# Infini-attention with a gating MLP: three units of stacks, maxima seven steps ahead, two products of w1 ahead, gates in one transfer

## The chip, the cores and the metric

The kernel runs on one core of a Trainium2 chip. A core has five engines that run side by side, each with its own stream of instructions in order: TensorE (PE in the profile, with its weight loads as PEld), VectorE (DVE), ScalarE (ACT), GpSimd (POOL) and SyncE (SP), which here only issues transfers (DMAs). The metric is the device time of one launch in microseconds; several runs are taken and their median counts.

## The reference, cut to what matters

```python
def _A_ref(x, wq, wk, wv, wo, beta):            # x: 1 x 2048 x 512
    H = 32; Dh = 16; N = 4; L = 512             # 4 segments of 512 rows
    q, k, v = (x @ w split into 32 heads and 4 segments, for w in wq, wk, wv)
    g = _sigmoid(beta)                          # one gate per head
    for s in range(N):
        p = _softmax(qs @ ks.T * Dh**-0.5 + causal mask)
        a_dot = p @ vs
        a_mem = (phi(qs) @ M) / (phi(qs) @ z + 1e-6)
        outs.append(g * a_mem + (1 - g) * a_dot)
        M += phi(ks).T @ vs;  z += sum(phi(ks))  # phi(t) = t + 1 if t > 0 else exp(t)
    return concat(outs) @ wo

def _B_ref(x, w1, w2):                           # 512 -> 1792 -> 512
    return max(x @ w1, 0) @ w2

xn = _layernorm(x)
return x + _A_ref(xn, ...) * _silu(_B_ref(xn, w1, w2))
```

## The kernel before

**Numbers.** Each dense product is made of three matmuls on operands split into a rounded part (h) and the rest (l): h·h, h·l, l·h. `triple` (L791) issues such a product, `lanes` (L744) cuts each of its matmuls into two of 64 rows, a lower and an upper one, which run on the two halves of the array side by side. The upper halves are held back: they trail the lower ones by up to `BACK` = 14 matmuls, so a chain of products ends 14 steps after its last lower half. The planner counts 0.69 us (`M3`) for a triple. ACT makes the rounded part of a weight (L475), POOL the rest (L476).

**Work.** The 2048 rows are 4 segments; the 512 columns of a segment's q or k are 4 groups of 8 heads, so there are 16 groups n, each in two units u = 2n + q of 4 heads, 32 units in all.

- `proj` (L1004) makes q and k of a group; `projout` (L1017) splits them and writes them to DRAM planes sdq and sdk (L1031, L1032): 0 or -1, then h and l.
- `stack` (L1161) loads a unit's planes into one of `NS` = 4 pairs of buffers QS and KS, one transfer of 512 KB each (L1167). In them one matmul over 64 rows gives the logits of a head.
- `rowmax` (L1179), five steps per unit: PE makes logits (L1193), DVE takes the maximum of each row over the causal part in one operation that also has to write its elements somewhere: it writes them back into the PSUM bank (L1199). `maxrows` (L1212): POOL splits the maxima (L1207, L1208), DVE transposes them (L1217), SP sends them to DRAM (mx, L1219) and from there into the free rows of the unit's QS (L1220).
- `expo` (L1229), five steps per unit: PE makes the logits again, transposed and now less their maximum (L1245), ACT the exponentials P (L1262, L1256), POOL clears the part above the diagonal (L1252). `pv` (L1275) multiplies by v (L1291) and ACT scales the result by 1 - g (F, L1306, with gsc).
- `memory`, `memory2`, `spread`, `numden` keep M and z and make the memory's share; its numerator is scaled by g (L1084, L1087, with gcol). `combine` (L1329) sends the denominators through DRAM for their reciprocals (cr, rq, dd, ee) and adds both shares (L1358 to L1363).
- `w1chain` (L807): one of 14 products f of 128 hidden columns, then hh on ACT (L819) and hl on DVE (L820), in rings of `NH` = 4 buffers. `w2chains` (L831) takes them in parts of 3 (the last part has 2), four chains of 128 rows, and adds into bacc (L870, L872). In `filler` (L1428) the w2 chains of a part follow the w1 product number `LOOK` = 1 of the next part.
- `gates` (L428): g from beta in two layouts, gcol (128 x 4) and gsc (128 x 8), loaded by 8 and 4 transfers (L430, L433), then tanh on ACT (L445, L446) and small steps on DVE (L447, L450, L451).
- `wipe` (L856) writes zeros with POOL into buffers whose last readers are lower halves: rows of xh and xl in the last segments, and at the end (L1621) whatever weight or hl buffer is marked in `lowread`.

**Order.** `emit` walks over steps t from -18 to 160. In each it spends a budget of filler work (w1, w2, v, layer norm, the output product), then issues `rowmax` of step t + `LAG` (9), more filler, then `expo` of step t; the exponentials of unit u start at step 5u. For group n, with T = 10n, `proj` is made urgent at T - 17 and the two stacks go out at T - 14 and T - 8. PE's stream is issued as it comes; the operations of ACT, DVE, POOL and SP are put in order by a planner (`Sched`, L73), which runs a model of the engines: each operation has a duration, a latency and a due time, and the engine that is free takes the ready operation that is due first. `await_` (L1507) pushes filler to PE until what a step needs is there by the model. The whole is planned several times, and the order that ends first by the model is the one that is built (`search`, L244). The model of the maxima is

```python
dve(w + 80, [pk, "causal"], ..., lambda ...: DVE.tensor_tensor_reduce(
    pS[:, o:o + w], pS[:, o:o + w], causal[:, L - w:], 1.0, -3.0e38, OP.add, OP.max, md[...]), 4.6)
```

that is 0.14 us and 1.05 ns for each of w + 80 columns. A transfer counts 0.63 us on SP and 2.2 us or a stated time until it has landed.

## Time and profile before

| | |
|---|---|
| median of 3 runs | 779.08 us (777.58, 779.08, 782.65) |
| profiled execution | 777.05 us, span 775.3 us, mean granted clock 0.985 |
| busy share of the span | PE 95%, DVE 63%, ACT 55%, POOL 53% |
| chain that ended last | PE 66%, DMA 15%, DVE 6%, issue 4%, ACT 4%, POOL 4% |
| transfers | 139.87 MB, 127074 packets, 26296 of them under 512 B |
| queue of SP | 56.5% of 16 DMA engines over the span |

The profile names an instruction by its line, engine and tiles (out<-in, buffer numbers left out). A wait "A <- B" is idle time of A that ended when B was done; the three numbers are the total in us, how often, and the longest. SPq and ACTq are the issues of transfers on these engines. Stages are read by their busy time per engine, followed by the clock granted to TensorE (1.00 is full), the share of the DMA engines and the rate.

### The profile page before, as it was taken

What the parts mean: (1) busy time and instruction counts of PE and PEld (TensorE: products, weight loads), DVE (VectorE), ACT (ScalarE), POOL (GpSimd) and SP (SyncE); (2) the same over time, 40 slices, a digit from 0 to 9 for tenths busy, and PEclk for the clock granted to TensorE, in tenths of its full rate; (3) what the DMA queues carried; (4) which work ended last, traced back from release to release, by engine and by line L of the source; (5) the groups of instructions that cost most, each with busy time, mean ns of one, the idle gap of its engine ahead of it and who ended that gap; (6) DMA issues with size and microseconds to landing.
All of it is one profiled execution on the core that took longest, in us unless ns stands there. A gap on an engine that the chain in (4) does not pass through costs nothing.

```text
span 775.3 us, 18578 instructions
## 1 busy us (share of the span) xinstructions
PE 734.1 (95%) x6832; PEld 573.3 (74%) x6832; DVE 486.0 (63%) x1489; ACT 422.8 (55%) x646; POOL 414.0 (53%) x508
## 2 busy tenths in 40 slices
PE   9979999999999999989899989989899999999997
PEld 8868877677777668756687759767666977766776
DVE  3115888588676876456676876367786556684344
ACT  3434455567676565445565765356556456766511
POOL 2734344354555355563664554573838557657652
PEclk9999999999999999989999999999999999999989
DMA  4565754556665456665466556656665847743413
GB/s 134 179 191 178 259 189 136 162 202 195 220 213 176 154 183 196 200 198 142 150 226 221 166 187 221 209 172 194 203 187 180 281 162 251 230 122 90 115 33 109
DMA packets 127074, 139.87 MB, mean 180 GB/s; under 512 B 26296, under 2 KB 71608, under 8 KB 126984
## 3 DMA queue, kind: packets, MB, share of 16 engines
q1 hardware_dynamic: 126776, 138.49, 56.5%
q8 instruction: 54, 0.88, 0.5%
q14 instruction: 36, 0.29, 0.1%
q10 hardware_dynamic: 208, 0.20, 0.1%
HBM read 99.00 MB, written 34.93 MB: 173 GB/s over the span
## 4 chain that ended last, share of the span: by engine, by line
PE 66%; DMA 15%; DVE 6%; issue 4%; ACT 4%; POOL 4%; SPq 1%; POOLq 0%; ACTq 0%; DVEq 0%
PE ps L775 35%; PE ps L784 9%; PE ps L1291 7%; PE pt L1245 4%; DMA sdq<-qkl 4%; PE ps L1193 4%; DMA sdk<-qkl 3%; DVE ps L1199 2%; PE pt L545 2%; DMA gcol<-in_A_beta_dram 2%; DMA ee<-rq 2%; ACT P L1262 1%; PE ps L1075 1%; DVE qkl L1028 1%; DMA io<-in_B_w_dram 1%
## 5 line engine op out<-in xcount | busy, mean ns | idle before, releaser
L476 POOL TENSOR_TENSOR wl<-io,wh 128x512 fp32r<-128x512 f32 x176 | 226.9, 1299 | 148.0 <-ACT wh L475 126.1
L1199 DVE CUSTOM_DVE_ANT_0 ps<-ps,causal 128x256 f32<-128x256 f32 (+3 forms) x512 | 244.0, 510 | 85.9 <-PE ps L1193 66.0
L1262 ACT ACTIVATE P<-pt 128x1024 f32<-128x1024 f32 x128 | 131.1, 1024 | 60.0 <-PE pt L1245 58.4
L1252 POOL TENSOR_SCALAR_AFFINE_SELECT P<-P 128x512 f32<-128x512 f32 x128 | 80.0, 636 | 120.0 <-ACT P L1262 91.7
L775 PE MATMUL ps<-xh,wh 64*128 64x512 f32 x352 | 141.4, 402 | 2.5 <-DVE md L1199 1.7
L784 PE MATMUL ps<-xl,wh 64*128 64x512 f32 x352 | 141.5, 402 | 0.0
L475 ACT ACTIVATE wh<-io 128x512 fp32r<-128x512 f32 x176 | 107.6, 628 | 58.4 <-PE ps L784 28.2
L784 PE MATMUL ps<-xh,wh 64*128 64x512 f32 x352 | 139.1, 395 | 0.0
L784 PE MATMUL ps<-xh,wl 64*128 64x512 f32 x352 | 137.8, 391 | 0.0
L775 PE MATMUL ps<-xh,wl 64*128 64x512 f32 x352 | 137.3, 390 | 0.0
L775 PE MATMUL ps<-xl,wh 64*128 64x512 f32 x352 | 137.0, 389 | 0.0
L775 PE MATMUL ps<-wh,hh 64*128 64x512 f32 x224 | 93.2, 416 | 12.7 <-ACT hh L819 8.6
L784 PE MATMUL ps<-wl,hh 64*128 64x512 f32 x224 | 92.5, 413 | 0.0
L775 PE MATMUL ps<-wh,hl 64*128 64x512 f32 x224 | 90.6, 404 | 0.9 <-DVE hl L820 0.8
L775 PE MATMUL ps<-wl,hh 64*128 64x512 f32 x224 | 89.2, 398 | 0.0
L784 PE MATMUL ps<-wh,hh 64*128 64x512 f32 x224 | 88.4, 395 | 0.0
L784 PE MATMUL ps<-wh,hl 64*128 64x512 f32 x224 | 88.3, 394 | 0.0
L1245 PE MATMUL pt<-qs,ks 64*128 64x128 f32 (+3 forms) x512 | 80.5, 336 | 6.9 <-ACT P L1262 6.8
L1193 PE MATMUL ps<-ks,qs 64*128 64x256 f32 (+3 forms) x512 | 76.8, 326 | 3.8 <-DVE hl L820 2.6
L1291 PE MATMUL ps<-P,vt 128*17 128x512 f32 (+3 forms) x1024 | 75.1, 434 | 1.7 <-POOL P L1252 1.7
L775 PEld LDWEIGHTS ps<-xh,wh 64*128 64x128 f32 x352 | 65.0, 185 | 12.8 <-DVE md L1199 4.4
L1199 DVE DVE_READ_ACCUMULATOR2_ANT md<- 128x1 f32 x512 | 72.1, 141 | 0.0
(175 smaller groups left out, 1789.4 us busy)
## 6 DMA issues: line engine op xcount, KB each, us to landing
io<-in_B_w_dram SPq DMA_DIRECT2D x112, 256.0 KB
qs<-sdq SPq DMA_DIRECT2D x32, 512.0 KB
ks<-sdk SPq DMA_DIRECT2D x32, 512.0 KB
sdq<-qkh SPq DMA_DIRECT2D x16, 512.0 KB
sdk<-qkh SPq DMA_DIRECT2D x16, 512.0 KB
io<-in_A_x_dram SPq DMA_DIRECT2D x28, 256.0 KB
io<-in_A_wv_dram SPq DMA_DIRECT2D x16, 256.0 KB
io<-in_A_wq_dram SPq DMA_DIRECT2D x16, 256.0 KB
```

The source lines that it names most:

```text
L475: act(512, [rk], [hk], lambda: ACT.activation(h, raw, AF.Copy), 7.0 + nsplit if early else 6.0)
L476: pool(512, [rk, hk], [lk], lambda: POOL.tensor_tensor(l, raw, r32(h), op=OP.subtract), 8.5 + 1.3 * nsplit if early else 25.4)
L545: PE.matmul(pw[:, :128], ident, ident, start=True, stop=True)
L775: i = PE.matmul(m[0], m[2][0][LO], m[2][1][LO], start=m[4], stop=False)
L784: PE.matmul(h[0], h[2][0][HI], h[2][1][HI], start=False, stop=h[5] is not None)
L1028: dve(512, [pk, thk], [tlk], lambda: DVE.tensor_tensor(tl, pp, r32(th), op=OP.subtract), 7.0)
L1193: PE.matmul(two[a][0][:, o:o + w], qs[r, p, w - 128:w], ks[r, p, :w], start=True, stop=True)
L1199: dve(w + 80, [pk, "causal"], [f"{dk}.{p}{a}{j}"], lambda p=p, j=j, o=o, w=w, a=a, pS=pS: DVE.tensor_tensor_reduce(pS[:, o:o + w], pS[:, o ...
L1245: PE.matmul(pT[:, a, o:o + w], ks[r, p, 128 * i:128 * i + 128], qs[r, p, 128 * i:], start=True, stop=True)
L1252: pool(512, ks, ks, lambda: POOL.affine_select(t, t, pattern=[[0, 4], [1, 128]], compare_op=OP.is_ge, fill=0.0, base=0, channel_multiplier ...
L1262: act(1024, tk, [both[p]], lambda: ACT.activation(P[:, 2 * p:2 * p + 2, :], pT, AF.Exp, scale=0.25), 18.5)
L1291: PE.matmul(pO[32 * b:32 * b + 17, 128 * i:], v, P[:, b, o:o + w], start=i == 0, stop=i == 3)
```

## The change

Constants: `NH` 4 to 5, `LOOK` 1 to 2, `NS` 4 to 3, `LAG` 9 to 7; new are `LOAD` = 0.11, `STACK` = (-10, -5) and `TTR` = 60.

- One unit of QS and KS less, and the stacks of a group go out at T - 10 and T - 5. The maxima run seven steps ahead of the exponentials, not nine.
- The w2 chains of a part follow the second w1 product of the next part; hh and hl have five buffers.
- The planner counts 0.11 us more until PE can use another engine's result.
- The gates come by one transfer: beta, repeated to all 128 partitions (bt, 128 x 32). One tanh on ACT, then eight small DVE operations (`picks`) choose gcol and gsc by masks made from blk.
- The maxima's operation writes its elements to a BF16 buffer in SBUF (none), and counts as 20 more columns.
- `wipe`, `retire` and `lowread` go.

```diff
-NH = 4
-LOOK = 1
+NH = 5
+LOOK = 2
-NS = 4
+NS = 3
-LAG = 9
+LAG = 7
+LOAD = 0.11
+STACK = (-10, -5)
+TTR = 60
...
             if d.eng != "PE":
-                s = max(s, d.t)
+                s = max(s, d.t + LOAD)
...
             if o is not None and o.eng != "PE":
-                t = max(t, o.t if o.out else self.now + 3.54)
+                t = max(t, o.t + LOAD if o.out else self.now + 3.54)
...
+    none = cst.tile([128, L], BF16, name="none")
...
     def gates():
-        for h in range(8):
-            dma((), [f"gcol{h}"], lambda h=h: SP.dma_start(gcol[16 * h:16 * h + 16], bass.AP(
-                tensor=beta.tensor, offset=beta.offset + h, ap=[[0, 16], [8, 4]])), 55.2)
-        for b in range(4):
-            dma((), [f"gsc{b}"], lambda b=b: SP.dma_start(gsc[32 * b:32 * b + 32], bass.AP(
-                tensor=beta.tensor, offset=beta.offset + b, ap=[[0, 32], [4, 8]])), 35.9)
+        dma((), ["bt"], lambda: SP.dma_start(bt, bass.AP(
+            tensor=beta.tensor, offset=beta.offset, ap=[[0, 128], [1, H]])), 10.0, 4.0)
...
+        def picks():
+
+            DVE.tensor_scalar(bt, bt, 0.5, 0.5, op0=OP.mult, op1=OP.add)
+            DVE.tensor_tensor(pick2, blk[:, 0::32], blk[:, 16::32], op=OP.add)
+            DVE.tensor_tensor(pick1, bt.rearrange("p (c h) -> p c h", h=8),
+                              blk[:, 0::16][:, None, :].to_broadcast([128, 4, 8]), op=OP.mult)
+            DVE.tensor_reduce(gcol, pick1, axis=AX.X, op=OP.add)
+            DVE.tensor_tensor(pick3, bt.rearrange("p (c b) -> p c b", b=4),
+                              pick2[:, None, :].to_broadcast([128, 8, 4]), op=OP.mult)
+            DVE.tensor_reduce(gsc, pick3, axis=AX.X, op=OP.add)
+            DVE.tensor_scalar(gsc, gsc, -1.0, 1.0, op0=OP.mult, op1=OP.add)
+            DVE.tensor_scalar(gsc, gsc, par[:, 1:2], par[:, 0:1], op0=OP.mult, op1=OP.add)
+
         dve(400, ["pari"], ["pari", "par"], parity, 54.1)
-        act(10, gk, gk, lambda: ACT.activation(gcol, gcol, AF.Tanh, scale=0.5), 62.2)
-        act(10, sk, sk, lambda: ACT.activation(gsc, gsc, AF.Tanh, scale=0.5), 77.5)
-        dve(10, gk, gk, lambda: DVE.tensor_scalar(gcol, gcol, 0.5, 0.5, op0=OP.mult, op1=OP.add), 76.6)
...
+        act(10, ["bt"], ["bt"], lambda: ACT.activation(bt, bt, AF.Tanh, scale=0.5), 62.2)
+        S.pend["ACT"][-1].dur = 1.6
+        dve(1000, ["bt", "blk", "par"], ["bt", "gcol", "gsc"], picks, 74.7)
...
-                dve(w + 80, [pk, "causal"], [f"{dk}.{p}{a}{j}"], lambda p=p, j=j, o=o, w=w, a=a, pS=pS: DVE.tensor_tensor_reduce(
-                    pS[:, o:o + w], pS[:, o:o + w], causal[:, L - w:], 1.0, -3.0e38, OP.add, OP.max,
+                dve(w + 40 + TTR, [pk, "causal"], [f"{dk}.{p}{a}{j}"], lambda p=p, j=j, o=o, w=w, a=a, pS=pS: DVE.tensor_tensor_reduce(
+                    none[:, :w], pS[:, o:o + w], causal[:, L - w:], 1.0, -3.0e38, OP.add, OP.max,
...
-            if t == T - 14:
+            if t == T + STACK[0]:
...
-            if t == T - 8:
+            if t == T + STACK[1]:
                 stack(n, 1)
...
-    for t, k in (*WH.t, *WL.t, *HLO.t):
-        if k in lowread:
-            wipe(t, [k])
```

## The prediction, made before the change was run

> **What bounds the kernel now.** I read the page first, then the waits of PE in three stretches, then stages of 20 us, then the places.

> ```profile
> span 775.3 us, 18578 instructions
> PE 734.1 (95%) x6832; PEld 573.3 (74%) x6832; DVE 486.0 (63%) x1489; ACT 422.8 (55%) x646; POOL 414.0 (53%) x508
> ...
> PE ps L775 <- ACT hh L819: 4.6, 1, 4.6
> PE ps L1122 <- ACT bacc L870: 1.7, 1, 1.7
> PE ps L775 <- DVE hl L820: 0.5, 1, 0.5
> ...
> PE pt L1245 <- ACT P L1262: 6.8, 7, 2.8
> PE ps L775 <- DVE md L1199: 4.7, 9, 1.1
> ...
> PE ps L775 <- ACT hh L819: 2.3, 3, 0.9
> ...
> PE ps L775 <- DVE hl L820: 0.3, 1, 0.3
> ...
> PE ps L775 <- ACT hh L819: 1.8, 1, 1.8
> ```

> The first three waits lie in 20 to 70 us, the next four in 70 to 740, the last in 740 to 776 (total us, times, longest). PE is busy 95% of the span and no other engine passes 63%, so PE's stream sets the time: what can be won is its idle 41.2 us (775.3 - 734.1), and the stretches in which it is busy at a low clock. The stages show these:

> ```profile
> 40.00:60.00 20.00, 14.12 (x108) 11.37 (x104) 3.65 (x8) 6.63 (x12) 5.06 (x4) 0.91 0.67 201
> ...
> 340.00:360.00 20.00, 19.86 (x166) 14.80 (x168) 10.60 (x37) 10.79 (x17) 8.02 (x13) 0.84 0.34 106
> 360.00:380.00 20.00, 16.29 (x122) 11.35 (x122) 13.98 (x42) 11.56 (x18) 13.59 (x15) 0.91 0.74 233
> ...
> 740.00:760.00 20.00, 18.20 (x94) 13.84 (x91) 11.37 (x20) 5.52 (x11) 8.14 (x13) 0.83 0.09 22
> ```

> Columns: stretch, length, busy PE, PEld, DVE, ACT, POOL, then granted clock, DMA share, GB/s. A clock of 0.91 over 20 us is 1.8 us of full-speed work lost, 0.84 is 3.2, 0.83 is 3.4. So the opening (40 to 62) loses 4.6 + 0.5 + 1.7 idle and 1.8 by the clock, 8.6 in all; the tail (746 to 756) loses 1.8 idle and 3.4 by the clock, 5.2 in all.

> **Gates by one transfer.** Why PE stands in the opening, and below it two pairs of mx transfers (units 23 and 31 of the 32), each with the last md before it and the first exponential behind it:

> ```profile
> GB/s 154 332 261 336 362 220 204 290 369 235 89 1 0 0 0 0 0 50 263 403 366 173 25 172 342 332 318 308 251 76 154 340 52 264 328 344 391 352 332 206
> ...
> gcol<-in_A_beta_dram SPq DMA_DIRECT2D x8, 0.2 KB
> gsc<-in_A_beta_dram SPq DMA_DIRECT2D x4, 1.0 KB
> ...
> 44.98 1.28 ACT L446 ACT_TABLE_LOAD   x1 [7.73 <-DMA gsc<-in_A_beta_dram]
> ...
> 60.12 0.21 ACT L445 ACTIVATE gcol<-gcol 128x4 f32<-128x4 f32 x1 [5.09 <-DMA gcol<-in_A_beta_dram]
> ...
> 46.73 0.29 DVE L451 TENSOR_SCALAR gsc<-gsc,par 128x8 f32<-128x8 f32 x1
> ...
> 551.02 0.14 DVE L1199 DVE_READ_ACCUMULATOR2_ANT md<- 128x1 f32 x1
> ...
> 556.84 0.41 SPq L1219 DMA_DIRECT2D mx<-mT  x1
> ...
> 561.71 0.59 SPq L1220 DMA_DIRECT2D qs<-mx  x1
> ...
> 567.51 0.50 PE L1245 MATMUL pt<-qs,ks 64*128 64x512 f32 x2
> ...
> 700.57 0.14 DVE L1199 DVE_READ_ACCUMULATOR2_ANT md<- 128x1 f32 x1
> ...
> 701.90 0.33 SPq L1219 DMA_DIRECT2D mx<-mT  x1
> ...
> 703.91 0.59 SPq L1220 DMA_DIRECT2D qs<-mx  x1
> ...
> 713.90 0.50 PE L1245 MATMUL pt<-qs,ks 64*128 64x512 f32 x2
> ```

> The first row is the DMA rate of 25 to 66 us in 40 slices: from 36 to 42 us next to nothing moves. A gsc transfer of 1 KB is 256 pieces of 4 bytes, one of gcol 64, and all else on the queue stands behind them. ACT takes its instructions in order: at L446 it stands 7.73 us, and behind it hh (L819), for which PE then waits 4.6; at L445 it stands 5.09 us, and behind it bacc (L870), for which PE waits 1.7. The change sends 128 rows of 128 bytes once. That is the shape of an mx transfer, whose hop from its issue to the issue that needs it took 2.0 us (701.90 to 703.91) and 4.9 us (556.84 to 561.71). The planner allows 4.0 and 0.63 of issue for it, so ACT waits between 0 and 0.3 us, and the table load of 1.28 us, which the planner had not counted, is in the 1.6 that it now counts. Eleven issues leave SP. On DVE eight small operations (picks) come in; at 0.2 to 0.3 us each, as L451, that is 1.6 to 2.4 us where 0.6 stood. Nothing reads them before the first scaled output (F), and DVE is busy for 3.65 of the 20 us from 40 to 60; without that cover they cost 1.8. I take the whole opening but 0.4: **-8.2** (bounds -4, if another late input stops ACT at the same place, and -8.6).

> **w1 two products ahead of w2.** Today the w2 chains of a part start when one w1 product of the next part is through, and the last hh that they need ends within them, since the upper halves trail by up to 14 steps where a product has 12. Hence L775's waits on hh and hl of 2.3 + 0.3 us in mid-run. In the tail w1 of f = 13 is followed at once by w2 of f = 12 and 13:

> ```profile
> 747.44 0.58 ACT L819 ACTIVATE hh<-ps 128x512 fp32r<-128x512 f32 x1
> ...
> 748.07 0.49 PE L775 MATMUL ps<-wh,hh 64*128 64x512 f32 x1 [1.80 <-ACT hh L819]
> ...
> 753.43 0.62 PE L775 MATMUL ps<-wl,hh 64*128 64x512 f32 x1
> 753.86 0.62 PE L775 MATMUL ps<-wh,hl 64*128 64x512 f32 x1
> ...
> 748.07 3.85 PE ps L775 x9
> ```

> With LOOK = 2 the w2 chains of f = 9 to 11 stand between, 12 triples of 0.69 us by the planner's figure: 8 us of cover for 0.6 us of hh and as much of hl. In mid-run it is one more product, four triples, 2.8 us. The fifth hh buffer holds three old products and two new ones and adds no wait. Behind the stall the matmuls come 0.43 us apart (753.43, 753.86), the half clock of the stage of 740 to 760. The last row is from the chain that ended last: it runs through PE here, so stall and clock both count. **-5.2** in the tail, **-2.6** in mid-run (bounds -1.8 and -5.2; 0 and -2.6, if the bank waits on md, 4.7 us today, take the place).

> [...]

> **Stacks later, in three units.** A step is the spacing of the exponentials:

> ```profile
> L1245 PEld LDWEIGHTS pt<-qs,ks x512: 182/184/335, 89.1 to 722.0; 64*128 64x128 f32 x171
> ...
> SPq L1167 <- DMA sdk<-qkl: 32.9, 13, 4.8
> ...
> SPq L1167 <- DMA sdq<-qkl: 18.3, 10, 3.4
> ...
> POOL pq L1360 <- DMA ee<-rq: 24.0, 9, 5.0
> ```

> 160 steps in 632.9 us are 3.96 us each. The two stack issues move from 14 and 8 steps before a group to 10 and 5, 16 and 12 us later, while their maxima move only 8 us later. SP stands 51 us today in stack issues whose sdq or sdk writes have not landed (longest 4.8); four steps later they have. What is queued behind them on SP, the ee and dd loads, the mx pairs and the weights, starts sooner. POOL's 24.0 us for ee stand on that queue, and behind POOL ACT's output copies and then PE's 6.8 for P. Bounds 0 and -6.8; I take **-2**, since the three hops of ee itself stay. With three units a stack waits for the exponentials of three units before, which end one step before it is issued, and it has three steps (12 us) until its maxima; two transfers of 512 KB at some 290 GB/s (the rates of 25 to 66 us reach 250 to 400) take 3.6 us, with a hop of 2 to 5. **0**; if SP came 4 us late, about 1 us a unit.

> **Maxima seven steps ahead.** The maxima of a unit must pass POOL (mm), DVE (mT) and two transfers before its first exponential. From the end of the last md in the rows above, unit 31 has 3.2 us to the second issue and 13.2 to the exponential; unit 23 has 10.6 and 16.4, with POOL and SP both late. Today no wait of PE names such a transfer. Two steps fewer take 7.9 us in the mean, and 5 to 7 in the tight units, whose exponentials stand 12 to 17 us apart. Read so for all 32 units (the first exponential at 89.1, the last unit's at 713.90), with 2.8 us for the second hop, three come late, by 6.4 us together; with 5.0, as in unit 23's first hop, six, by 15. The planner fills waits that it foresees with w1 and w2 work, and a stack no longer goes out beside the mx pair. So **+3**, bounds 0 and +15.

> **Maxima's junk in BF16.** The trace has no such form; the nearest are these, and the third row is of the next point:

> ```profile
> L1199 DVE CUSTOM_DVE_ANT_0 ps<-ps,causal 128x512 f32<-128x512 f32 x128 | 86.7, 711 | 53.8 <-PE ps L1193 39.9 <-ACT F L1306 12.2 <-PE ps L784 1.3
> ...
> L872 DVE TENSOR_TENSOR bacc<-ps,bacc 128x512 f32<-128x512 f32 x64 | 43.7, 683 | 24.0 <-PE ps L784 23.6
> ...
> L858 POOL MEMSET hl<- x2: 522/522/523, 772.4 to 772.8; 128x512 f32 x2
> ```

> Written to SBUF, the 512 wide one should go from 711 to about 683 ns as L872 has it; the planner's figure goes up by 21 ns instead. 512 of them are -14 to +11 us of DVE, an engine busy 63%; PE feels it only where it waits for a bank (md, nine times in mid-run), 0.03 us each. **0**, bounds -0.3 and +0.3. Late waits counted in the order (0.11 us): 16 waits of PE in mid-run on md and P and as many smaller ones, so 0 to -3.5; I take **0**, as the new order brings waits of its own. The memsets that fall away (L858, 0.52 us each) end at 773.3, under the last stores, 2.0 us before the span does: **0**, bounds 0 and -0.5.

> **Sum.** -8.2 - 5.2 - 2.6 - 2 + 3 = -15.0 on the profiled execution's 777.05 us (775.3 of span and 1.75 around it): 762.0. The median shown, 779.08, is 2.0 higher, so a median should read **764.0**.

> **The rivals.**
> 1. *Stalls come back elsewhere.* The planner makes a new order for all 775 us, and the mid-run waits are drawn anew. For it: the clock fell twice around 340 to 370 (3.2 + 1.8 us) behind waits that the order did not foresee. Against: SP is freer. Two more stalls of 2.8 us (the longest wait on P) with 3.4 us of clock behind each: 764 + 12.4 = 776.
> 2. *The maxima come too late, slower.* If the 3.6 us of a stack's two transfers lie ahead of the mx pair in most units, 12 of the 32 come late, by 31 us together by the same reading; the rest still gains, so 764 - 3 + 31 = 792. It decides from about 2.5 us more per chain, where the lateness reaches the 18 us won elsewhere. For it: unit 23, whose pair left behind two stack issues. Against: the stacks now leave two steps before the pair.
> 3. *The freed SP queue reaches PE.* All 6.8 us for P and the 5.0 us of clock at 340 to 380 go: 764 + 2 - 11.8 = 754.

> **How the numbers follow.** Forecast 0.60, rival 1 0.21, rival 2 0.07, rival 3 0.12. A measurement of this kernel tells about 1% (7.8 us) from no change, so faster begins at 771.3. The forecast and rival 3 lie there, and a little of rival 1: faster 0.74, same 0.19, slower 0.07. The likeliest alone spans 758 to 771; the range 753 to 777 takes in rivals 1 and 3 and leaves out rival 2 and the outer parts.

> **What would show it.** Right: ACT's waits on gsc and gcol gone and no dead stretch in the DMA rate of the opening; clock 1.00 there and in the tail; PE's waits on hh from 8.7 to under 2 us; SP's waits of the stack issues from 51 to under 20; the 512 wide maxima near 683 ns. Wrong: PE or PEld at L1245 waiting on qs<-mx, or at L1193 on a stack; the clock down at two places or more in mid-run; ACT standing on bt as it stood on gsc.

## The result, and the profile after

The changed kernel took **746.18 us** (median of four runs, 743.21 to 749.30) against 778.35 us for the kernel before in the same measurement: a ratio of 0.958, 95% interval 0.952 to 0.963. The prediction had the direction right and named 764, with a range of 753 to 777; the result lies 7 us below that range. The profiled execution took 743.21 us, 33.8 less than the one of before, where the prediction's sum was -15.0.

The head of the page of the changed kernel, and stages of it in the columns of the prediction:

```profile
span 741.1 us, 18738 instructions
PE 715.0 (96%) x6840; PEld 557.6 (75%) x6840; DVE 484.9 (65%) x1494; ACT 424.1 (57%) x645; POOL 410.6 (55%) x500
PEclk9999999999999999999999999999999999999999
```

```profile
40.00:60.00 20.00, 20.00 (x178) 17.26 (x175) 7.87 (x19) 9.87 (x19) 7.34 (x14) 1.00 0.90 293
...
340.00:360.00 20.00, 20.00 (x192) 14.69 (x188) 16.67 (x56) 15.81 (x25) 12.62 (x14) 1.00 0.81 271
360.00:380.00 20.00, 19.14 (x214) 14.20 (x214) 16.55 (x48) 13.14 (x20) 14.25 (x19) 1.00 0.58 171
540.00:560.00 20.00, 17.00 (x140) 12.51 (x138) 12.20 (x37) 10.31 (x16) 7.97 (x10) 0.91 0.77 240
```

The opening is full: 178 matmuls in 40 to 60 us where there were 108, the clock at 1.00, the DMA share at 0.90. The two stages of 340 to 380 us, at 0.84 and 0.91 before, run at 1.00. One low stage is left in mid-run, at 540 to 560.

Idle PE fell by only 15.1 us (41.2 to 26.1), though the span fell by 34.2; busy time itself fell by 19.1 us, with eight matmuls more. So the busy row hides part of what was won. How it does so shows at one stall of the kernel before, first in the timeline of PE, then in that of its weight loads (start, us, engine, line, operation, tiles, and in brackets the idle time before it):

```profile
135.22 0.40 PE L775 MATMUL ps<-wh,hh 64*128 64x512 f32 x1
...
135.45 0.39 PE L775 MATMUL ps<-wl,hh 64*128 64x512 f32 x1
...
136.14 0.50 PE L775 MATMUL ps<-wh,hl 64*128 64x512 f32 x1 [0.29 <-DVE hl L820]
...
136.48 0.39 PE L775 MATMUL ps<-xh,wh 64*128 64x512 f32 x1
```

```profile
136.14 0.18 PEld L775 LDWEIGHTS ps<-wh,hl 64*128 64x128 f32 x1 [0.73 <-DVE hl L820]
```

In full work the matmuls of the lower half start 0.23 us apart (135.22, 135.45), each recorded with 0.39. Here the next start comes 0.69 us later, and the one behind it 0.34: 0.46 and 0.11 us are lost, 0.57 in all. PE's idle time says 0.29, the weight load says 0.73. So PE's view is 0.44 us shorter than the weight loads' for this stall, and by that a stall that they show with under 0.44 is not in it at all; they overstate the loss by 0.16. (The stall at 587.60 us, shown further down, gives 0.43 and 0.16 by the same reckoning.) Here are their waits (total us, times, longest), the kernel before first:

```profile
PEld pt L1245 <- ACT P L1262: 12.9, 16, 3.2
PEld ps L775 <- ACT hh L819: 11.0, 7, 4.9
PEld ps L775 <- DVE md L1199: 10.4, 20, 1.4
PEld ps L775 <- DVE hl L820: 6.8, 14, 1.1
...
PEld ps L1193 <- DVE hl L820: 3.5, 2, 2.0
```

The kernel after; L1233, L782, L1187 and L824 are the old L1245, L775, L1199 and L820:

```profile
PEld pt L1233 <- ACT P L1250: 10.2, 10, 3.0
PEld ps L782 <- DVE md L1187: 7.8, 14, 1.2
...
PEld pt L1233 <- DMA qs<-mx: 1.5, 2, 1.0
...
PEld ps L782 <- DVE hl L824: 0.3, 1, 0.3
```

Waits on hh and hl were 21.3 us in the kernel before (11.0 + 6.8 + 3.5) and are 1.1 now (0.3 and two of 0.4 on other lines). The prediction had found 9.5 us of them, because it read them as idle time of PE (8.7 on hh, 0.8 on hl). In 70 to 740 us, where it took 2.3 + 0.3, the weight loads waited 12.6. This is their view of that stretch:

```profile
PEld ps L775 <- DVE hl L820: 5.2, 12, 0.7
...
PEld ps L775 <- ACT hh L819: 3.9, 5, 1.3
PEld ps L1193 <- DVE hl L820: 3.5, 2, 2.0
```

and PE's own row for the last of them, which the prediction did not read because it stands under the maxima's line:

```profile
PE ps L1193 <- DVE hl L820: 2.6, 2, 1.6
```

Of the twelve waits on hl at L775, PE's view had kept one, with 0.3 us.

**The whole account.** Adding every line of the weight-load waits except those on "issue" (short gaps between instructions, 49.3 us before and 47.5 after, nearly the same in all orders but one below) gives 79.0 us before and 52.9 after: -26.1. The trace's clock record gives the time at half clock before the last matmul; half of that is lost, by the record's clock of 0.50 (lower matmuls start 0.43 us apart there, 753.43 and 753.86, not 0.23): 10.2 us before, in stretches that start at 49, 340, 367 and 749 us, and 1.7 after, at 552: -8.5. Together that is -34.6, beside -34.2 us of span. What is left of the time up to the last matmul (770.5 and 737.0) is 681.3 and 682.4 us. There are 123 such waits before and 89 after; if each is overstated by the 0.16 of the stall above, the waits give -21 of the -34 and the rest -4. This account is used for all runs below; each is of one profiled execution, which for a_look1 was one of 781.57 us, well above its median, so that its clock is not compared.

### The profile page after: what moved, and what is told of

The parts are those of the page before. It is cut to its first block, busy times and chain, and to the rows that moved or that the text cites. A ratio compares the mean times of both kernels' runs of the same rounds, so it can differ in the third digit from the quotient of the medians.

```text
span 741.1 us, 18738 instructions
## 1 busy us (share of the span) xinstructions
PE 715.0 (96%) x6840; PEld 557.6 (75%) x6840; DVE 484.9 (65%) x1494; ACT 424.1 (57%) x645; POOL 410.6 (55%) x500
## 4 chain that ended last, share of the span: by engine, by line
PE 67%; DMA 14%; DVE 7%; POOL 4%; issue 3%; SPq 2%; ACT 2%; DVEq 0%; POOLq 0%; ACTq 0%
PE ps L782 40%; PE ps L791 7%; PE ps L1279 6%; PE pt L1233 4%; PE ps L1181 4%; DVE none L1187 2%; DMA io<-in_B_w_dram 2%; DMA out_dram<-io 2%; PE pt L553 2%; DMA sdq<-qkl 2%; DMA rq<-cr 2%; DMA ee<-rq 2%; POOL wl L485 1%; SPq L1303 1%; PE ps L678 1%
## 5 line engine op out<-in xcount | busy, mean ns | idle before, releaser
L1187 DVE CUSTOM_DVE_ANT_0 none<-ps,causal 128x256 bf16<-128x256 f32 (+3 forms) x512 | 250.4, 489 | 95.6 <-PE ps L1181 67.0
L782 PE MATMUL ps<-xh,wh 64*128 64x512 f32 x352 | 140.9, 400 | 2.2 <-DVE F L1077 1.5
L782 PE MATMUL ps<-xl,wh 64*128 64x512 f32 x352 | 137.2, 390 | 0.0
L782 PE MATMUL ps<-xh,wl 64*128 64x512 f32 x352 | 137.0, 389 | 0.0
L782 PE MATMUL ps<-wh,hh 64*128 64x512 f32 x224 | 89.7, 400 | 2.9 <-DVE md L1187 2.8
L791 PE MATMUL ps<-wl,hh 64*128 64x512 f32 x224 | 90.1, 402 | 0.0
L782 PE MATMUL ps<-wl,hh 64*128 64x512 f32 x224 | 87.1, 389 | 0.2 <-POOL wl L485 0.2
L791 PE MATMUL ps<-wh,hl 64*128 64x512 f32 x224 | 87.0, 389 | 0.0
L782 PE MATMUL ps<-wh,hl 64*128 64x512 f32 x224 | 86.9, 388 | 0.0
L791 PE MATMUL ps<-wh,hh 64*128 64x512 f32 x224 | 86.9, 388 | 0.0
L1233 PE MATMUL pt<-qs,ks 64*128 64x128 f32 (+3 forms) x512 | 77.8, 332 | 7.2 <-ACT P L1250 6.1
L1181 PE MATMUL ps<-ks,qs 64*128 64x256 f32 (+3 forms) x512 | 75.1, 324 | 3.8 <-DVE md L1187 1.1
L782 PEld LDWEIGHTS ps<-xh,wh 64*128 64x128 f32 x352 | 65.2, 185 | 14.9 <-DVE md L1187 2.9
L782 PEld LDWEIGHTS ps<-xh,wl 64*128 64x128 f32 x352 | 65.1, 185 | 11.4
```

The lines of the kernel that those rows point to most:

```text
L782: i = PE.matmul(m[0], m[2][0][LO], m[2][1][LO], start=m[4], stop=False)
L791: PE.matmul(h[0], h[2][0][HI], h[2][1][HI], start=False, stop=h[5] is not None)
L1181: PE.matmul(two[a][0][:, o:o + w], qs[r, p, w - 128:w], ks[r, p, :w], start=True, stop=True)
L1187: dve(w + 40 + TTR, [pk, "causal"], [f"{dk}.{p}{a}{j}"], lambda p=p, j=j, o=o, w=w, a=a, pS=pS: DVE.tensor_tensor_reduce(none[:, :w], pS[: ...
L1233: PE.matmul(pT[:, a, o:o + w], ks[r, p, 128 * i:128 * i + 128], qs[r, p, 128 * i:], start=True, stop=True)
```

## The experiments

Each edit below is made in one of the two kernels and the planner then makes its own order, so that every edit is also a new draw of the order. Ratios are to the kernel before, measured beside each. The last four columns come from the profile of each: waits of the weight loads, hh and hl among them, clock loss, and the rest up to the last matmul.

| kernel | median, us | ratio (95%) | waits | hh, hl | clock | rest |
|---|---|---|---|---|---|---|
| before | 778.35 | 1 | 79.0 | 21.3 | 10.2 | 681.3 |
| b_gates | 770.74 | 0.988 (0.984 to 0.992) | 71.4 | 12.7 | 8.5 | 681.7 |
| b_lag7 | 773.99 | 0.994 (0.991 to 0.997) | 75.8 | 14.3 | 13.7 | 679.8 |
| b_look2 | 765.98 | 0.984 (0.978 to 0.990) | 60.5 | 6.3 | 15.4 | 684.2 |
| b_sw42 | 781.12 | 1.003 (0.999 to 1.008) | 78.9 | 16.6 | 20.5 | 676.9 |
| b_back8 | 786.68 | 1.011 (1.003 to 1.018) | 39.6 | 2.5 | 3.4 | 737.5 |
| after | 746.18 | 0.958 (0.952 to 0.963) | 52.9 | 1.1 | 1.7 | 682.4 |
| a_psum | 745.79 | 0.953 (0.948 to 0.958) | 56.0 | 1.9 | 6.8 | 683.4 |
| a_load0 | 749.45 | 0.959 (0.954 to 0.964) | 51.7 | 3.6 | 5.1 | 685.9 |
| a_load13 | 749.48 | 0.963 (0.954 to 0.971) | 53.4 | 0.7 | 6.8 | 681.2 |
| a_sw42 | 757.81 | 0.974 (0.967 to 0.981) | 61.2 | 1.5 | 10.2 | 684.1 |
| a_lag8 | 762.80 | 0.977 (0.972 to 0.981) | 58.1 | 1.8 | 13.7 | 685.8 |
| a_oldgates | 767.78 | 0.983 (0.978 to 0.987) | 65.2 | 6.2 | 10.2 | 687.3 |
| a_oldgates_l13 | 753.55 | 0.970 (0.963 to 0.978) | 59.3 | 5.3 | 3.4 | 681.7 |
| a_oldgates_l0 | 761.32 | 0.981 (0.974 to 0.988) | 63.2 | 4.5 | 5.1 | 685.9 |
| a_look1 | 773.70 | 0.993 (0.990 to 0.996) | 71.1 | 14.8 | 17.1 | 687.3 |
| a_look1_l13 | 785.61 | 1.008 (1.003 to 1.013) | 83.3 | 15.0 | 13.7 | 685.2 |
| a_look1_l0 | 761.48 | 0.979 (0.973 to 0.986) | 70.9 | 14.3 | 0.0 | 685.1 |

The rest is 677 to 687 us in 17 of the 18 kernels: an order is as good as its waits and its clock. In b_back8, the exception, the gaps put down to "issue" are 110.7 us instead of some 50.

### Single parts, put into the kernel before

**b_gates**: the gates alone.

```diff
-        for h in range(8):
-            dma((), [f"gcol{h}"], ...)
-        for b in range(4):
-            dma((), [f"gsc{b}"], ...)
+        dma((), ["bt"], lambda: SP.dma_start(bt, ... ap=[[0, 128], [1, H]]), 10.0, 4.0)
...
+        dve(1000, ["bt", "blk", "par"], ["bt", "gcol", "gsc"], picks, 74.7)
```

> The kernel before with the gates alone changed (one transfer, one tanh, eight small steps). Theory: the opening loses 8.6 us to the twelve transfers (6.8 idle, 1.8 by the clock), so 8 us less than before, a ratio near 0.990, and no dead stretch in the DMA rate. Rival (the whole order was merely drawn luckily): any time within 8 us of before on either side, with the opening stall replaced by another of ACT there.

-9.6 us by the ratio. The stage of 40 to 60 us of this kernel, and then its wait on hh over the whole run (L780 and L824 are the old L775 and L819):

```profile
40.00:60.00 20.00, 19.76 (x172) 16.49 (x171) 7.76 (x25) 9.66 (x17) 7.56 (x6) 1.00 0.83 266
```

```profile
PEld ps L780 <- ACT hh L824: 6.1, 7, 2.1
```

PE is busy 19.76 of 20 us instead of 14.12, at a clock of 1.00 instead of 0.91, and the longest wait on hh is 2.1 instead of 4.9. In 20 to 70 us the waits on hh, hl and bacc, 8.2 us in the kernel before, are down to 0.6 us. The gates alone are worth about what the prediction gave them, and for its reason.

**b_lag7**: stacks later and maxima seven steps ahead, with four units still.

```diff
-LAG = 9
+LAG = 7
...
-            if t == T - 14:
+            if t == T - 10:
...
-            if t == T - 8:
+            if t == T - 5:
```

> The kernel before with its four units, but the stacks at T - 10 and T - 5 and the maxima seven steps ahead. Theory (the gain behind the 15 us forecast lies in w1 being two products ahead): within 4 us of before, ratio 0.995 to 1.005, SP's waits for sdq and sdk at the stacks gone, but PE's waits behind hh and hl as large as before. Rival (the freed queue of SP carries the surplus): 10 us or more faster, ratio 0.987 or less.

-4.8 us by the ratio, 0.8 more than the theory allowed: not the +1 that the prediction's -2 and +3 make, and far from rival 2. The way is not the one that was argued, though. The waits on P, which the later stacks were to shorten, grew from 12.9 to 17.8 us, while the waits on hh and hl, which the theory held to stay, fell from 21.3 to 14.3 (in mid-run from 12.6 to 6.4) with one product ahead as before. So this -4.8 may be the new order as much as the edit. PE does come to wait for the maxima's transfer, but little; this is that wait, and behind it SP's wait at the stacks for their writes, which was 32.9 + 18.3:

```profile
PEld pt L1245 <- DMA qs<-mx: 1.3, 3, 0.7
```

```profile
SPq L1167 <- DMA sdk<-qkl: 5.3, 3, 3.2
```

**b_look2**: the same, with three units, five buffers and two products ahead (two products ahead were not tried beside four units).

```diff
-NH = 4
-LOOK = 1
+NH = 5
+LOOK = 2
-NS = 4
+NS = 3
...                 (LAG and the stacks as in b_lag7)
```

> The kernel before with three units, stacks at T - 10 and T - 5, maxima seven steps ahead, five hh buffers and w1 two products ahead; old gates, old maxima form, old planner figures. Theory: PEld's waits behind hh and hl in mid-run and the tail (12.4 us), the tail's clock (3.4) and upper halves that run alone (1.8) go, the opening stays: 15 to 18 us faster, about 761, ratio 0.977 to 0.981. Rival (gates and planner figures carry it): less than 8 us.

-12.5 us by the ratio, 7.6 more than b_lag7 and short of the 15 to 18 of the theory. Its waits on hh and hl fall from 14.3 to 6.3, although its gates are the old ones:

```profile
PEld ps L775 <- DVE hl L820: 5.1, 4, 3.0
...
PEld ps L775 <- ACT hh L819: 1.2, 1, 1.2
```

In total waits the parts come to the sum: gates -7.6, stacks and maxima -3.2, two products ahead -15.3 (60.5 against 75.8) make -26.1, which is what the whole change took. It is partly chance. Of the -15.3 only -8.0 are waits on hh and hl, and b_gates and b_look2 both shorten the same stall of the opening: with the old gates ACT still stands 6.6 and 4.9 us for them in b_look2, but PE's waits before 70 us are 4.1 us, where b_lag7 has 7.7. In time the parts don't add up: the two halves of the change make -9.6 - 12.5 = -22, the whole -33. b_look2 lost 15.4 us by the clock, the changed kernel 1.7.

### Where the waits on hh came from

**b_back8**: the kernel before, its upper halves trailing by 8 steps at most.

```diff
-BACK = 14
+BACK = 8
```

> The kernel before, w1 still one product ahead, but the upper halves trail by 8 matmuls instead of 14, so the last hh of a part ends 1.4 us earlier. Theory (the mid-run waits behind hh and hl come from that trail): PEld's waits behind hh and hl fall from 21.3 to 12 us or less, the opening's and the tail's stay, 3 to 10 us faster if the new order costs nothing. Rival (they come from late engines, not from the trail): 18 us or more of such waits.

Slower, by 8.3 us at the measured ratio of 1.011. Its weight-load waits:

```profile
PEld ps L784 <- issue: 62.4, 114, 0.6
...
PEld ps L775 <- DVE hl L820: 1.2, 4, 0.4
...
PEld ps L775 <- ACT hh L819: 1.1, 1, 1.1
```

The waits on hh and hl fell from 21.3 to 2.5, without any second product ahead. That fits the trail: the last hh and hl of a product that a w2 chain needs end 14 steps late, and the chain starts after 12. The price stands in the first line, at the upper halves (L784): an upper chain must not start before its lower one has ended, and with 8 steps it now stood in front of that 114 times for some 0.55 us (the profile names no releaser; that it is this fence is read from the code). LOOK = 2 buys the same cure without that price.

By itself this run does not refute the rival of late engines. Its expectation was wrong on the gain of 3 to 10 us and on the waits of the opening, which did not stay; and PE stands 62.4 us elsewhere now, which gives ACT and DVE more time as well. The trace of the kernel before decides it. Here is one of its mid-run stalls, from the product's last upper half on:

```profile
586.24 0.39 PE L784 MATMUL ps<-xh,wl 64*128 64x512 f32 x1
...
586.96 0.59 ACT L819 ACTIVATE hh<-ps 128x512 fp32r<-128x512 f32 x1
...
587.58 0.69 DVE L820 SCALAR_TENSOR_TENSOR hl<-ps,hh 128x512 fp32r<-128x512 f32 x1 [0.59 <-ACT hh L819]
587.60 0.18 PEld L775 LDWEIGHTS ps<-wh,hh 64*128 64x128 f32 x1 [1.17 <-ACT hh L819]
```

The product ends at 586.63, hh starts 0.33 us later and hl directly behind hh. The 19 mid-run waits stand behind 14 products. For 12 of them the trace names the end on PE that ACT waited for, and hh started within 0.45 us of it; in 13 of the 14 hl started within 0.6 us of the end of hh. One hl, at 114.72, came 3.1 us late. So the trail, and not a late engine, makes these waits in all but that case, and a delay of some tenths adds to some of them.

### Single parts, taken out of the changed kernel

**a_psum**: the maxima's junk back into the PSUM bank, planned alike.

```diff
-                dve(w + 40 + TTR, [pk, "causal"], ...
-                    none[:, :w], pS[:, o:o + w], causal[:, L - w:], ...
+                dve(w + 80, [pk, "causal"], ...
+                    pS[:, o:o + w], pS[:, o:o + w], causal[:, L - w:], ...
```

> The changed kernel in the same order, but the maxima write their elements back into the PSUM bank, in F32, as before. Theory: the order is the same, so 128x512 goes back from 688 to about 711 ns and the time stays within 3 us of the changed kernel's 746. Rival (the SBUF target shortens what PE waits for at the banks): 4 us slower or more, PEld's waits behind md up from 13.6 to 17 us.

No change of time (0.953 against 0.958, intervals overlapping). The maxima of the changed kernel, and below them those of a_psum:

```profile
L1187 DVE CUSTOM_DVE_ANT_0 none<-ps,causal 128x512 bf16<-128x512 f32 x128 | 88.0, 688 | 31.2 <-PE ps L1181 23.4
...
L1187 DVE DVE_READ_ACCUMULATOR2_ANT md<- 128x1 f32 x512 | 42.4, 83 | 0.0
```

```profile
L1187 DVE CUSTOM_DVE_ANT_0 ps<-ps,causal 128x512 f32<-128x512 f32 x128 | 86.0, 709 | 27.1 <-PE ps L1181 26.8
L1187 DVE DVE_READ_ACCUMULATOR2_ANT md<- 128x1 f32 x512 | 72.0, 141 | 0.0
```

709 to 688 ns is near what the prediction had (711 to 683). The fall of the read of the result, 141 to 83 ns in 512 places, it had not. DVE was not the bound, and neither shows in the time. The operations of DVE, ACT, POOL and SP stand in the same order in both profiles, and still the one of a_psum (752.39 us, its slowest run) lost 6.8 us by the clock and the other 1.7: so far can executions of one order lie apart.

**a_load0, a_load13, a_sw42, a_lag8**: neighbours of the changed kernel.

```diff
-LOAD = 0.11
+LOAD = 0.0          (a_load0)
+LOAD = 0.13         (a_load13)
-SWITCH = 0.40
+SWITCH = 0.42       (a_sw42; the planner's time of a change of moving operand)
-LAG = 7
+LAG = 8             (a_lag8)
```

> The changed kernel without the 0.11 us for late waits in the planner, so another order. Theory: the 0.11 us are worth 0 to 4 us, 744 to 751. Rival (the margin is what keeps the new order free of stalls): 8 us slower or more, with PE's waits and half-clock windows as numerous as before the change.

> The changed kernel with LOAD 0.13 in place of 0.11, a second draw of the order. Theory: anywhere from 744 to 764. Rival (the edits fix the time): within 4 us of the changed kernel's 746.

> The changed kernel with a planner figure that no edit touched (SWITCH 0.40 to 0.42), so another order of the same work. Theory (the order that was built is one draw among many, worth several us of waits and half-clock windows): anywhere from 744 to 764. Rival (the edits fix the time): within 4 us of the changed kernel's 746.

> The changed kernel with the maxima eight steps ahead, so one step more for the chain of the maxima and one less for the stacks. Theory: the chain hardly costs anything at seven (1.5 us of PEld behind qs<-mx), so within 4 us of the changed kernel, qs<-mx waits gone. Rival (the forecast's +3 to +15 for late maxima is there, hidden in other waits): 5 us faster or more.

LOAD is worth 3 us at most, within what the draw does. a_sw42 changes no part of the change and is 11.6 us slower than the changed kernel; a_lag8 is 16.6 slower, which neither theory had: its waits on qs<-mx are gone as expected, but all waits together are 5.2 longer, 4.3 of it on P, and the clock lost 12.0 more. a_sw42 shows the scatter of the order; for a_lag8, run in one order, it is not shown how much of the 16.6 is that and how much the eighth step. In the kernel before, the edit of a_sw42 moved the time by +2.6 us by the ratio, which the interval (0.999 to 1.008) does not tell from nothing:

> The kernel before with SWITCH 0.42, another order of the same work. Theory (draws of the order scatter on both sides): anywhere from 768 to 788. Rival (the kernel before is an unlucky draw, and the surplus of the gain is that): 768 or less.

The four orders that keep every part (after, a_load0, a_load13, a_sw42) take 746 to 758 us, 750.7 in the mean; the changed kernel is the best of the four. About 4 of the 18 us by which the prediction was too high are therefore a good draw.

**a_oldgates and a_look1**, each in three orders (LOAD 0.11, 0.13 and 0).

```diff
-        dma((), ["bt"], ...)
+        for h in range(8): ...        (gates and their readers as before: a_oldgates)
...
-LOOK = 2
+LOOK = 1                              (a_look1)
...
-LOAD = 0.11
+LOAD = 0.13                           (the runs with _l13; 0.0 in those with _l0)
```

> The changed kernel with the twelve small gate transfers, two tanh and three small steps of before. Theory (the parts add up as PE's weight-load waits): 7 to 10 us slower than the changed kernel, 753 to 756, with ACT standing 5 us or more on gsc or gcol and the DMA rate near nothing for 6 us. Rival (with w1 two products ahead PE has enough work to cover the opening): within 3 us of the changed kernel.

> The changed kernel with w1 one product ahead again; the fifth buffer of hh stays. Theory: 14 to 18 us slower than the changed kernel, 760 to 764, ratio to before 0.977 to 0.982, with PEld's waits behind hh and hl at 10 us or more and the tail's stall and half clock back. Rival (the fifth buffer, the stacks or the new planner figures carry it): within 5 us of the changed kernel's 746.

Both cost more than they are worth alone and more than their theories had, 19 and 28 us by the ratios. Chance of the order, or parts that strengthen each other? The further orders were run for that.

> The changed kernel with the gates read as before (seven strided reads), planned with LOAD at 0.13 instead of 0.11, so that the order is another draw. Beside it stands the changed kernel at LOAD 0.13, 749.5 us. Theory (the gates are worth the same 8 to 10 us as alone in the kernel before, and the 21 us of the first draw hold a chance of the order): 757 to 762 us. Rival (in the changed kernel the gates are worth more, since a late start of the gates upsets the whole run): 768 to 772 us.

> The changed kernel with the gates read as before, planned with LOAD at 0. Beside it stands the changed kernel at LOAD 0, 749.5 us. Theory (8 to 10 us and a chance of the order): 757 to 762 us. Rival (worth 20 us and more here): 768 to 772 us.

> The changed kernel with w1 one product ahead of w2 (LOOK at 1), planned with LOAD at 0.13. Beside it stands the changed kernel at LOAD 0.13, 749.5 us. Theory (the second product ahead takes the 13 to 15 us of weight-load waits on hh and hl away, the rest of the 27 us of the first draw is a chance of the order): 763 to 768 us, hh and hl waits of 12 to 17 us. Rival (the second product ahead is worth more than its waits, by the half-clock stretches behind them): 773 to 778 us.

> The changed kernel with LOOK at 1, planned with LOAD at 0. Beside it stands the changed kernel at LOAD 0, 749.5 us. Theory (13 to 15 us of waits and a chance of the order): 763 to 768 us, hh and hl waits of 12 to 17 us. Rival (worth 24 us and more): 773 to 778 us.

Against the kernel of the same LOAD the old gates cost 2.5, 0.8 and 2.2% (19, 6 and 17 us), 14 us in the mean, where they were worth 9.6 alone. One of the two further orders lies in the theory's range, the other below it, and neither near the rival's: a chance of the order, as far as two orders tell. (The old gates are twelve transfers, not seven as one expectation says.) What the opening itself shows of them is less than the 9.6: with two products ahead ACT still stands over 11 us for the gates, but PE's waits before 70 us are 4.5 to 5.1 us instead of 1.8, and the clock there loses 0 to 3.4. One product ahead cost 3.6, 4.6 and 2.1% (28, 36 and 16 us), and here neither forecast holds: one order is beyond the rival's, the other just under the theory's. What does hold in all three is the wait that the theory named:

```profile
PEld ps L782 <- DVE hl L824: 8.8, 15, 1.5
...
PEld ps L782 <- ACT hh L823: 5.4, 9, 1.1
```

```profile
PEld ps L782 <- DVE hl L824: 7.4, 14, 0.8
...
PEld ps L782 <- ACT hh L823: 6.2, 10, 1.4
```

The first pair is of a_look1_l13, the second of a_look1_l0. With the rest of these waits, on other lines, they are 15.0 and 14.3 us (14.8 in a_look1), against 0.7 to 3.6 with two products ahead. Yet the two take 785.6 and 761.5 us. The difference is in the other waits (12 us more, on pk and bacc among others) and in the clock: 13.7 us lost in the one, none in the other, though that one has 70.9 us of waits too. Whether two products ahead are worth more here than the 15 us of waits (the mean of three orders says 26, b_look2 against b_lag7 says 8) is left open; three orders that scatter by 20 us do not settle it.

## Why the prediction was wrong in size

Its terms beside the account of the two profiled executions, in us:

| term | predicted | measured |
|---|---|---|
| opening, gates | -8.2 | -9.9 (waits on hh, hl and bacc 8.2, clock 1.7; two products ahead shorten the same stall) |
| two ahead, tail | -5.2 | -6.0 (waits 2.6, clock 3.4) |
| two ahead, mid-run | -2.6 | -11.5 (12.6 to 1.1) |
| clock in mid-run | 0 | -3.4 (5.1 lost at 340 to 370, now 1.7 at 552) |
| stacks later | -2 | -2.7 (waits on P 12.9 to 10.2) |
| maxima seven ahead | +3 | +1.5 (qs<-mx) |
| junk, late waits | 0 | -3.8 (waits on md 17.4 to 13.6; 15.8 in a_psum, the same order with the old form) |
| all other waits and the rest | 0 | +1.6 |
| sum | -15.0 | -34.2 of span |

**The step that failed** is the size of "two ahead, mid-run". The mechanism was right, stated in the prediction itself (the upper halves trail by 14 steps where a product has 12), and the trace of the kernel before, b_back8 and the three a_look1 runs bear it out. But the price was read off PE's idle time, 2.3 + 0.3 us, without the 2.6 that stood under L1193, and in a view that leaves out some 0.44 us of each stall. The weight loads waited 12.6 us there in 19 places; at 0.16 less for each that is still 9.6 us lost. The bound "0 and -2.6" was therefore no bound. The term is 8.9 of the 19.2 us by the table, about 6 with the 0.16 taken off. Part of that is the draw of the order before: in the seven orders with one product ahead and the long trail these waits are 6.4 to 12.6 us, 9.9 in the mean, and the kernel before is the highest; with two ahead they are 0.7 to 3.9.

**The clock** was the second miss. The prediction put the 5.0 us at 340 to 380 into rival 3 with a chance of 0.12 and had a new order lose as much as the old one. The reading of it, that a stall costs again by the clock behind it, was right (in the tail of the kernel before a stall of 1.80 us and then 6.83 us at half clock), and the new order, with 26 us fewer waits, falls to half clock at one place instead of four. The size of this term is in part luck of the profiled execution, the fastest of its four: in the profile of a_psum the same order lost 5.1 us in mid-run, as much as the kernel before. Rival 3 was otherwise wrong, since the waits on P largely stayed (6.8 to 6.1 us of PE's idle time). Rival 1 was right in its mechanism: a_sw42 and a_lag8 are orders in which waits and half-clock stretches came back, at 758 and 763 us. That the order that was built is not one of them is luck.

**Stacks and maxima** were forecast at +1 together and came to -1.2 in the table. Read from the tightest units, two steps fewer made 6.4 us of lateness; two units of 32 came late, by 1.5 together. Why so little is not shown. In b_lag7 SP stands 5.3 us in the stacks for a write instead of 51, but the mx pairs behind them hardly gain by it: from a unit's last md to its second issue it is 5.6 us in the median against 5.8 before. That the planner filled what it foresaw, as the prediction allowed, fits and was not tested. Of three units a wait remains that the prediction had put at nothing, SP's stacks waiting for a buffer's last readers, in the changed kernel:

```profile
SPq L1155 <- PE pt L1233: 14.2, 13, 2.3
SPq L1155 <- PE ps L1181: 9.7, 5, 3.1
...
SPq L1155 <- DMA sdk<-qkl: 5.1, 3, 3.6
```

So SP stands 29 us there, not under 20, but it costs PE nothing that its waits show. The -2.7 on P did not come by the way that was argued: in b_lag7 the waits on P grew, and POOL's wait for ee, which was to shrink, grew here from 24.0 us to this:

```profile
POOL pq L1348 <- DMA ee<-rq: 32.7, 9, 8.2
```

**Right as argued**: the opening, the tail, the junk and the late waits at next to nothing (a_psum, a_load0). The wipes were in no run of their own; from the last matmul to the end it is 4.1 us instead of 4.8. The picks took longer than given, one of the eight alone 1.07 us, under cover all the same. ACT's waits on the gates are gone:

```profile
33.27 0.68 SPq L437 DMA_DIRECT2D bt<-in_A_beta_dram  x1
```

```profile
L460 ACT ACT_TABLE_LOAD  x1: 1283/1283/1283, 38.7 to 38.7; - x1
L460 ACT ACTIVATE bt<-bt x1: 232/232/232, 40.0 to 40.0; 128x32 f32<-128x32 f32 x1
```

Issued at 33.27, used at 40.0, and no wait of ACT on bt stands in its list.

## What to carry to other kernels

Where one engine is 95% busy with pipelined work, price its stalls by the spacing of its starts or in the queue in front of it (here the weight loads), and take the rows of all lines that name the late result: the gaps in its busy time leave out the short stalls (here 0.29 us of idle where the weight load waited 0.73, and one of twelve waits on hl). In a kernel whose order is planned anew by every edit, one run of an edit carries the draw of the order with it (746 to 758 us here for the same parts); put the edit into two or three orders before you believe its size, and compare the waits it aims at, which separate more clearly than the time (here those on hh and hl: 12.7 to 21.3 us with one product ahead, 0.7 to 6.3 with two). A chain whose end is held back on purpose needs as much independent work behind it as it is held back, and here that was cheaper to add than to shorten the hold.

## What the runs showed of the hardware

```profile
336.12:339.53 3.41, 1.25 (x12) 0.69 (x8) 0.81 (x4) 0.99 (x2) 3.00 (x6) 0.99 0.50 149
339.53:342.94 3.41, 2.80 (x12) 1.84 (x14) 1.38 (x4) 2.95 (x5) 1.80 (x3) 0.50 0.71 233
...
363.43:366.84 3.41, 1.69 (x9) 0.67 (x7) 2.32 (x8) 1.44 (x3) 1.19 (x2) 0.99 1.02 228
366.84:370.25 3.41, 3.41 (x21) 3.02 (x20) 1.97 (x7) 1.71 (x2) 3.41 (x3) 0.51 1.07 377
370.25:373.66 3.41, 2.56 (x20) 1.60 (x21) 2.31 (x8) 2.67 (x4) 2.14 (x4) 1.00 0.51 193
```

Steps with 2.16 and 1.72 us idle are followed by one at half clock; the one with 0.85 us idle (370.25) is not. (At 342.94 a second step at half clock follows, behind one with 0.61 us idle that was itself at half clock.) Over 17 profiles (all but a_look1's), after the opening 28 us, a step at full clock was followed by a half-clock one in 43 of 44 cases where PE was idle for 1.75 us or more of it, in 10 of 20 between 1.5 and 1.75, in 11 of 97 between 1.0 and 1.5, and in 2 of 3364 below 1.0. (Before and after alone: 3 of 3, 2 of 4, none of 12, none of 396.) Idle is here what PE's own busy time leaves, with modelled ends of the matmuls. The phase of the grid differs from run to run (its first step begins 1.56 us into the span in the kernel before, 2.65 in the changed one), so the same waits may fall into one step or be split over two; that this makes the difference from run to run is argued, not tested. The four runs of the changed kernel fit it: 743.21 and 745.21 us at a mean clock of 0.997 and 0.998, 747.15 at 0.991, 749.30 at 0.986.

At 366.79 half clock came behind a step with 1.72 of its 3.41 us idle. The changed kernel's one half-clock step stands behind one with two gaps, of 1.20 and 0.39 us. By the counts above the stalls to avoid here are those of 1.5 us, or several smaller ones within one step.

**The read of an accumulated maximum** took 141 ns when the operation before it wrote to PSUM in FP32 and 83 when it wrote BF16 to SBUF (means of 512 each, a_psum and the changed kernel, same code otherwise).
